# One operand's transpose moved from the matrix engine to the DMA crossbar, with three loads held behind it

## The chip, the cores and the metric

One core of a Trainium2 chip. The metric is the device time of one execution in microseconds (us). Several executions are compared; a run is slow when it is over 1.5% above the fastest of its kernel. A ratio is the mean time of one kernel's fast runs over that of the other's fast runs of the same rounds, so it is not quite the ratio of the medians quoted beside it. The span in a profile (248.2 us for the kernel before) is a little shorter than the device time of the same run (249.99 us). Places in time are us from the start of the span.

Engines: PE is the matrix engine, DVE the vector engine, ACT the scalar engine, POOL the general engine (here it issues the loads and does some copies), SP the engine that issues the transposing DMA transfers and the output stores. "SPq" in a profile line is an instruction of SP's DMA issue. SBUF is the on-chip memory that the engines work from, PSUM the one that PE writes its results to (psA and ot in the profile lines), and "the crossbar" is short for the way of a transposing transfer (DMA_TRANSPOSE in the profile lines). A transfer has landed when its completion is signalled.

## The reference

Two attentions, then a gated two-layer product. Shapes: 8 batches, 8 heads, 576 rows, head size 64, 32 packed queries; the second part is 4608 x 512 with a hidden size of 2048.

```python
def sm_attn(qq, kk, vv):                      # softmax(scale * qq kk^T) vv
    ...
p_packed = sm_attn(p, k, v)                   # first attention: 32 packed queries a head
out      = sm_attn(q, p_packed, p_packed)     # second attention: 32 keys a head
x = out.transpose(0, 2, 1, 3).reshape(4608, 512)
h = x @ w_in
result = (h * cos(h)) @ w_out
```

## The kernel before

The kernel works batch by batch. For batch b it needs k and q with the head dimension on the partitions ("kT", "qT"), so both are transposed after loading. This is done in one of two ways: on PE, in three groups of eight transposes, each group copied out of PSUM by DVE, or by a transposing DMA through the crossbar, issued from SP. The attention weights of the first attention ("a1") are transposed too, in the same two ways.

Loads are issued from POOL and convert fp32 to bf16 on the way. Each moves 576 KB into SBUF.

"Slot s" is the stretch in which the hidden products of batch s run on PE (16 steps, "fc"), filled up with the output products of batch s - 1. "Hooks" put other work at given steps. Between two slots stand the scores of the next batches.

```python
def load(n, b):                                   # POOL issues; bf16 in SBUF
    bf[n, b] = bf_pool.tile(..., bufs=2 if n == "k" else 1)
    G.dma_start(out=bf[n, b], in_=srcs[n][b]...)

def xbar(n, b):                                   # transposing DMA, SP issues
    t = xT[n, b] = att_pool.tile([128, H * 3, TP], ..., bufs=2 if n == "k" else 1)
    nc.sync.dma_start_transpose(out=t, in_=bf[n, b]...)

def pe_T(n, b, engs, groups, own=False):          # 8 PE transposes a group, 1 copy
    ...
# --- cut: set-up and batch 0 ---
    a1_one(1)
    load("k", 2)
    permute_v(1)
    load("v", 2)
    for fc in range(NFC):                         # slot 0
        ...
# --- cut ---
    def tk(n, b, i):
        return lambda: pe_T(n, b, (V, V, V), (i,))

    def next_loads():                             # the gate: POOL reads one element of kT3,
        G.tensor_copy(out=gate, in_=xT["k", 3][0:1, 0, 0:1])   # so it stops until kT3 landed
        for n, b in (("q", 3), ("k", 4), ("v", 3)):
            load(n, b)
    ...
    s2(1)
    ppw(1, 0, V)
    load("q", 2)
    load("k", 3)
    dup_p(4, 2 * B, G)
    ...
    slot(1, [(3, ...), (4, lambda: (xbar("q", 2), xbar("k", 3))),
             (5, tk("k", 2, 0)), (6, tk("k", 2, 1)), (7, tk("k", 2, 2)),
             (9, ...), (11, ...), (12, next_loads)], 4, {3: 3})
    ...
    # --- of this stretch only the lines that matter here; fillers and others are cut ---
    s1(2)              # first scores of batch 2: need kT2
    a1_pe(2, ...)      # its attention weights transposed on PE
    pp(2)              # its pooled product a1 x v: needs v2
    s2(2)              # second scores of batch 2: need qT2
    s1(3)              # first scores of batch 3: need kT3
    xbar("q", 3)       # three transfers, in this order on SP
    a1_xbar(3)
    xbar("k", 4)
    ...
    slot(2, [(4, lambda: permute_v(3, V)), (7, lambda: pp(3, ...)), (11, ...)], 5, {11: 3})
```

The pooled product of batch 3, pp(3), is in slot 2. It needs v3 (unpacked on DVE by permute_v(3)) and a1T3, the transposed attention weights of batch 3. From slot 3 on the kernel repeats one pattern.

The softmax here doesn't subtract the row's maximum and nothing guards it: scores larger than these inputs give would overflow.

Of the kernel before, what the change touches and what calls it, by code (L numbers as in the profile page):

```python
# [15 lines left out]
def kernel(  # L16
# [38 lines left out]
    V, ACT, G = nc.vector, nc.scalar, nc.gpsimd  # L55
# [5 lines left out]
    gate = const.tile([1, 1], BF16, name="gate")  # L61
# [8 lines left out]
    bf, vp, xT, a1T, sums1, r1, rs1 = {}, {}, {}, {}, {}, {}, {}  # L70
    a2u, lns, a2n, PPW = {}, {}, {}, {}

    def copy(eng, out, in_):
        if eng is ACT:
            ACT.copy(out=out, in_=in_)  # L75
        else:
            eng.tensor_copy(out=out, in_=in_)  # L77

    def psa(dt=FP32):
        return A.tile([128, 2, 512 if dt == FP32 else 1024], dt, name="psA", tag="A")  # L80

    def load(n, b):
        bf[n, b] = bf_pool.tile([TP, H, C * D], BF16, name=n + "bf", tag=n + "bf", bufs=2 if n == "k" else 1)
        G.dma_start(out=bf[n, b], in_=srcs[n][b].rearrange("h (p c) d -> p h (c d)", c=C))

    def permute_v(b, eng=G):
        vp[b] = vp_pool.tile([TP, C, H * D], BF16, name="vp", tag="vp")
        copy(eng, vp[b].rearrange("p c (h d) -> p c h d", h=H),
             bf["v", b].rearrange("p h (c d) -> p c h d", c=C))

    def xbar(n, b):
        t = xT[n, b] = att_pool.tile([128, H * 3, TP], BF16, name=n + "T", tag=n + "T", bufs=2 if n == "k" else 1)
        nc.sync.dma_start_transpose(out=t, in_=bf[n, b].rearrange("p h x -> p (h x)"))

    def pe_T(n, b, engs=(V, V, V), groups=(0, 1, 2), own=False):
        if 0 in groups:
            xT[n, b] = att_pool.tile([128, H * 3, TP], BF16, name=n + "T", tag=n + "T", bufs=2 if n == "k" else 1)
        t = xT[n, b]
        flat = bf[n, b].rearrange("p h x -> p (h x)")
        for i in groups:  # L100
            ps = bank(BF16) if own else psa(BF16)[:, 0, :]
            for j in range(8):
                o = 8 * i + j
                nc.tensor.transpose(ps[:, j * TP:(j + 1) * TP], flat[:, o * 128:(o + 1) * 128],  # L104
                                    ident[0:TP, 0:TP])
            copy(engs[i], t[:, 8 * i:8 * i + 8].rearrange("p a x -> p (a x)"),
                 ps[:, 0:8 * TP])

    def bank(dt=FP32):
        return O.tile([128, 512 if dt == FP32 else 1024], dt, name="ot", tag="ot")  # L110

    def pack_p(b0, b1, flat=None):
        ng = 2 * (b1 - b0)
        if flat is None:
            flat = psa(BF16).rearrange("p a x -> p (a x)")
        for g in range(ng):
            nc.tensor.transpose(flat[:, g * 128:(g + 1) * 128],
                                p_bf[:, 2 * b0 + g].rearrange("p t d -> p (t d)"), ident)
        V.tensor_copy(out=P2[:, b0:b1].rearrange("p b h n -> p (b h n)"), in_=flat[:, 0:ng * 128])
# [75 lines left out]
    def ppw(b, n, eng=None, own=False, later=False, cuts=((0, 512),)):  # L195
        if b not in PPW:
            PPW[b] = ppw_pool.tile([128, 2, DF], BF16, name="PPW", tag="PPW")
        two = isinstance(eng, tuple)
        if own:
            ps = [bank(), bank()]  # L200
        else:
            t = psa()
            ps = [t[:, 0, :], t[:, 1, :]]
        for x in range(4):
            for y in range(2):
                r = slice(64 * y, 64 * y + 64)
                nc.tensor.matmul(ps[y][32 * x:32 * x + 32, :], ppT[b % 2][r, 2 * x + y, :],  # L207
                                 w_in_bf[r, x, n * 512:(n + 1) * 512], start=True, stop=True)

        def evacuate(cuts=cuts):  # L210
            if own or two:
                for a, z in cuts:
                    for y in range(2):
                        copy(eng[y] if two else eng, PPW[b][:, y, n * 512 + a:n * 512 + z], ps[y][:, a:z])
            else:
                copy(eng or (V, ACT)[n % 2], PPW[b][:, :, n * 512:(n + 1) * 512], t)
        if later:
            return [lambda c=c: evacuate((c,)) for c in cuts]
        evacuate()
# [8 lines left out]
    def sums2(b, y):  # L228
        if b not in lns:
            lns[b] = att_pool.tile([128, 2, S], FP32, name="lns", tag="lns")  # L230
        ps = psa()
        for e in range(2):
            nc.tensor.matmul(ps[:, e, 0:HS], ones_blk, a2u[b][:, y, e * HS:(e + 1) * HS],  # L233
                             start=True, stop=True)
        ACT.activation(out=lns[b][:, y].rearrange("p (e x) -> p e x", e=2),  # L235
                       in_=ps[:, :, 0:HS], func=AF.Ln)
# [11 lines left out]
    def h_mm(b, fc):  # L248
        if fc == 0:
            gT[b] = g_pool.tile([128, NFC, S], BF16, name="gT", tag="gT")  # L250
            if b % 2 == 0:
                joint[b // 2] = j_pool.tile([128, NFC, 128], BF16, name="joint", tag="joint")
        ps = psa()
        for y in range(2):
            for e in range(2):
                nc.tensor.matmul(ps[:, e, 0:HS], PPW[b][:, y, fc * 128:(fc + 1) * 128],  # L256
                                 a2n[b][:, y, e * HS:(e + 1) * HS], start=(y == 0), stop=(y == 1))
        cs = cos_pool.tile([128, S], BF16, name="cosT")
        csv = cs.rearrange("p (e x) -> p e x", e=2)
        ACT.activation(out=csv, in_=ps[:, :, 0:HS], func=AF.Sin, bias=PI_HALF)  # L260

        def rest():
            V.tensor_tensor(out=gT[b][:, fc, :].rearrange("p (e x) -> p e x", e=2),  # L263
                            in0=ps[:, :, 0:HS], in1=csv, op=ALU.mult)
            if fc % 8 == 7:
                j0 = (b % 2) * 64
                G.tensor_copy(out=joint[b // 2][:, fc - 7:fc + 1, j0:j0 + 64],  # L267
                              in_=gT[b][:, fc - 7:fc + 1, 512:576])
        return rest
# [56 lines left out]
    def fill(n):  # L326
        while n > 0 and filler[1] > 0:
            next(filler[0])
            filler[1] -= 1
            n -= 1  # L330
# [9 lines left out]
    def dup_p(a, b, eng):  # L340
        for t in range(2):
            eng.tensor_copy(out=p_bf[:, a:b, t, :], in_=p_raw[:, a:b, :])
# [57 lines left out]
    a1_one(1)  # L400
    load("k", 2)
    permute_v(1)
    load("v", 2)
    for fc in range(NFC):
        rest = h_mm(0, fc)
        if fc in (11, 12, 13):
# [13 lines left out]
    def slot(s, hooks, keep=0, heavy={}):  # L420
        left = filler[1] - keep
        out_eng[:] = (ACT,) if s > 1 else (V, ACT)
        weight = [1 + heavy.get(fc, 0) for fc in range(NFC)]
        for fc in range(NFC):
            h_mm(s, fc)()
            quota = (left * sum(weight[:fc + 1])) // sum(weight) - (left + keep - filler[1])
            first = quota
            while hooks and hooks[0][0] == fc:
                if first == quota and fc in heavy:
                    first = quota // 2  # L430
                    fill(first)
                hooks.pop(0)[1]()
            fill(quota - first if first != quota else quota)

    def pw2(b, n=0, eng=None):
        ppw(b, n, eng)
        ppw(b, n + 1, eng)

    def tk(n, b, i):
        return lambda: pe_T(n, b, (V, V, V), (i,))  # L440

    def next_loads():
        G.tensor_copy(out=gate, in_=xT["k", 3][0:1, 0, 0:1])
        for n, b in (("q", 3), ("k", 4), ("v", 3)):
            load(n, b)
# [2 lines left out]
    fill(4)  # L448
    s2(1)
    ppw(1, 0, V)  # L450
    load("q", 2)
    load("k", 3)
    dup_p(4, 2 * B, G)
    fill(5)
    sums2(1, 0)
    sums2(1, 1)
# [2 lines left out]
    normalise(1)  # L459
    ACT.preload_act_table_set(SIN_SET)  # L460
    fill(14)
    slot(1, [(3, lambda: pw2(1, 2, (ACT, V))), (4, lambda: (xbar("q", 2), xbar("k", 3))), (5, tk("k", 2, 0)), (6, tk("k", 2, 1)),
             (7, tk("k", 2, 2)), (9, lambda: pack_p(2, 5)),
             (11, lambda: pack_p(5, B)), (12, next_loads)], 4, {3: 3})

    ACT.preload_act_table_set(EXP_SET)
# [104 lines left out]
```

## Time and profile before

| what | value | where read |
|---|---|---|
| time | 249.91 us (median of the first 3 runs; 6 runs later: 249.81 to 250.28) | times |
| PE busy | 94% of 248.2 us | busy shares |
| granted PE clock | 1.00 | mean of the core |
| DMA | a queue of loads until about 58 us, about 205 GB/s | 40 slices, landings |

The profile page of the kernel before: the busy row of PE, and of the 40 slices the granted clock (9 is 90% or more), the mean busy share of the DMA engines and the GB/s they moved. A slice is 6.2 us.

```profile
...
PE 234.5 (94%) x2003; PEld 131.6 (53%) x2037; DVE 168.0 (68%) x254; ACT 166.9 (67%) x278; POOL 54.8 (22%) x68
...
PEclk9999999999999999999999999999999999999999
DMA  6999999999899999999989995989491113201133
GB/s 91 203 203 206 205 206 229 200 241 153 162 206 219 167 158 220 206 193 173 190 162 192 174 194 68 177 164 209 103 156 33 45 42 82 47 26 58 46 83 85
...
```

PE is the limit. The DMA row reads 9 from the second slice to the tenth (about 62 us), and mostly 8 or 9 well beyond. k2, v2, q2 and k3 took 20.0, 19.4, 16.4 and 18.6 us from issue to landing and landed one after the other, the last at 58.6 us, while the trio after the next gate took 6.8 to 12.6 us. Up to about 58 us, then, loads stand in a queue. The transfers issued by SP (start, duration of the issue on SP, out<-in):

```profile
...
55.70 3.96 SPq L93 DMA_TRANSPOSE qT<-qbf  x1
59.72 2.94 SPq L93 DMA_TRANSPOSE kT<-kbf  x1
...
72.11 5.98 SPq L93 DMA_TRANSPOSE qT<-qbf  x1
78.19 2.46 SPq L156 DMA_TRANSPOSE a1T<-a  x1
...
```

An issue's duration is not its landing. The trace's issue-to-landing times say that qT2 landed 5.4 us after 55.70, kT3 4.9 us after 59.72, qT3 10.4 us after 72.11 (two loads were still under way beside it), and a1T3 5.6 us after 78.19, at 83.8. POOL's gate on kT3:

```profile
...
64.70 0.18 POOL L443 COPY gate<-kT 1x1 bf16<-1x1 bf16 x1 [8.52 <-DMA kT<-kbf]
...
```

It opened at 64.70. Then q3, k4 and v3 were issued, and landed at 72.0, 75.7 and 79.4.

PE's timeline. First steps with and without a group of transposes (L256 opens each step; L104 is a group):

```profile
...
46.02 0.65 PE L256 MATMUL psA<-a2n,PPW 128*128 128x288 bf16 x4
...
46.94 0.65 PE L256 MATMUL psA<-a2n,PPW 128*128 128x288 bf16 x4
...
51.90 0.65 PE L256 MATMUL psA<-a2n,PPW 128*128 128x288 bf16 x4
52.60 0.50 PE L104 MATMUL psA<-ident,kbf 96*128 96x96 bf16 x8
...
53.38 0.65 PE L256 MATMUL psA<-a2n,PPW 128*128 128x288 bf16 x4
...
```

From 46.02 to 46.94 a plain step takes 0.92 us; from 51.90 to 53.38 a step with a group takes 1.48 us. Then the points:

```profile
...
63.89 0.44 PE L129 MATMUL psA<-kT,P 64*32 64x288 bf16 x16
...
69.77 0.44 PE L129 MATMUL psA<-qT,ppT 64*32 64x288 bf16 x16
...
71.54 0.44 PE L129 MATMUL psA<-kT,P 64*32 64x288 bf16 x16
...
78.07 0.41 PE L256 MATMUL psA<-a2n,PPW 128*128 128x288 bf16 x2
...
85.58 0.86 PE L183 MATMUL psA<-a1T,vp 96*128 96x64 bf16 x24 [0.58 <-DVE gT L263]
...
```

These are the first scores of batch 2 (kT2), its second scores (qT2), the first scores of batch 3 (kT3), the first hidden product of slot 2, and pp(3). No DMA is waited for at any of them. a1T3 had landed at 83.8, so it had 1.8 us to spare at 85.58.

### The profile page before, as it was taken

The numbers are of one execution on the slowest core, as the hardware profiler recorded it, in microseconds if no ns is written. First come the engines' busy times: TensorE is split into PE (matmuls) and PEld (weight loads), VectorE is DVE, ScalarE is ACT, GpSimd is POOL, SyncE is SP. The second block draws the span as 40 slices with busy tenths as digits, with TensorE's granted clock in tenths as the row PEclk, the third lists the DMA queues.
The fourth block names the chain that finished last, engine by engine and source line by source line (L and its number), as shares of the span: only waits on it lengthen the run. The fifth ranks groups of instructions, "written<-read, shape, count | busy, mean of one in ns | idle before, by whom it ended". The sixth has DMA issues, their size and how long they took to land.

```text
span 248.2 us, 5035 instructions
## 1 busy us (share of the span) xinstructions
PE 234.5 (94%) x2003; PEld 131.6 (53%) x2037; DVE 168.0 (68%) x254; ACT 166.9 (67%) x278; POOL 54.8 (22%) x68
## 2 busy tenths in 40 slices
PE   8878799999999899999999999999999999999993
PEld 3454374566544654475546554565456554665452
DVE  2549987789568967678857766678766774876110
ACT  2368799746566787888877777888787684873000
POOL 8333533240400044022313105030500000000000
PEclk9999999999999999999999999999999999999999
DMA  6999999999899999999989995989491113201133
GB/s 91 203 203 206 205 206 229 200 241 153 162 206 219 167 158 220 206 193 173 190 162 192 174 194 68 177 164 209 103 156 33 45 42 82 47 26 58 46 83 85
DMA packets 63175, 37.09 MB, mean 149 GB/s; under 512 B 35792, under 2 KB 58576, under 8 KB 63152
## 3 DMA queue, kind: packets, MB, share of 16 engines
q0 software_dynamic: 23152, 18.75, 49.5%
q1 hardware_dynamic: 39568, 17.83, 34.3%
q8 instruction: 16, 0.26, 0.4%
q10 hardware_dynamic: 432, 0.20, 0.4%
q14 instruction: 7, 0.06, 0.1%
HBM read 37.22 MB, written 9.44 MB: 188 GB/s over the span
## 4 chain that ended last, share of the span: by engine, by line
PE 75%; DMA 9%; DVE 7%; ACT 5%; issue 2%; SPq 0%; DVEq 0%; ACTq 0%
PE ot L309 42%; PE psA L256 19%; DMA qbf<-in_q_dram 7%; DVE gT L263 4%; PE psA L207 3%; PE ot L347 3%; PE psA L183 2%; ACT cosT L260 2%; DMA out_dram<-osb 2%; PE psA L129 2%; PE ot L295 1%; PE psA L233 1%; DVE PPW L77 1%; ACT ppT L75 1%; PE psA L104 1%
## 5 line engine op out<-in xcount | busy, mean ns | idle before, releaser
L309 PE MATMUL ot<-w_out_bf,gT 128*128 128x512 bf16 x482 | 127.4, 379 | 2.1 <-issue 1.3
L263 DVE TENSOR_TENSOR gT<-psA,cosT 128x576 bf16<-128x576 f32 x128 | 93.6, 755 | 26.5 <-ACT cosT L260 25.9
L260 ACT ACTIVATE cosT<-psA 128x576 bf16<-128x576 f32 x128 | 82.5, 652 | 28.0 <-PE psA L256 23.2
L256 PE MATMUL psA<-a2n,PPW 128*128 128x288 bf16 x512 | 83.8, 286 | 1.9 <-DVE PPW L77 0.4
L309 PEld LDWEIGHTS <-gT 128*128 128x128 bf16 x512 | 47.7, 98 | 43.2 <-issue 6.7
L256 PEld LDWEIGHTS <-PPW 128*128 128x128 bf16 x512 | 49.3, 98 | 35.2 <-issue 4.4
L77 DVE CAST PPW<-psA 128x1024 bf16<-128x1024 f32 (+1 forms) x23 | 26.9, 1176 | 11.6 <-PE psA L207 11.5
L267 POOL COPY joint<-gT 128x512 bf16<-128x512 bf16 x16 | 9.8, 614 | 88.5 <-DVE gT L263 88.5
L77 DVE COPY osb<-ot 128x512 f32<-128x512 f32 (+1 forms) x24 | 16.3, 679 | 17.5 <-PE ot L309 7.6
L75 ACT COPY osb<-ot 128x512 f32<-128x512 f32 (+1 forms) x13 | 7.3, 565 | 15.3 <-PE ot L309 10.6
L77 POOL COPY vp<-vbf 96x3072 bf16<-96x3072 bf16 x6 | 16.5, 2751 | 3.8 <-DMA vbf<-in_v_dram 3.8
L243 DVE SCALAR_TENSOR_TENSOR a2n<-a2u,r,lns 128x576 bf16<-128x576 bf16 x16 | 12.3, 814 | 7.3 <-ACT lns L241 7.3
L140 ACT ACTIVATE a<-psA 128x576 bf16<-128x576 f32 x16 | 10.3, 647 | 7.1 <-PE psA L129 7.1
L235 ACT ACTIVATE lns<-psA 128x576 f32<-128x576 f32 x16 | 10.2, 650 | 7.1 <-PE psA L233 6.5
L309 PE MATMUL ot<-w_out_bf,joint 128*128 128x512 bf16 x46 | 12.4, 379 | 0.1
L225 ACT ACTIVATE a2u<-psA,rs 128x576 bf16<-128x576 f32 x16 | 11.0, 737 | 1.4 <-PE psA L129 1.3
L75 ACT CAST ppT<-psA 64x128 bf16<-64x128 f32 x24 | 6.2, 260 | 7.2 <-DVE ppT L77 5.9
L207 PE MATMUL psA<-w_in_bf,ppT 64*32 64x512 bf16 x224 | 10.2, 381 | 0.0
L347 PE MATMUL ot<-wz 128*128 128x512 bf16 x23 | 8.7, 524 | 1.4 <-DVE wz L358 1.2
L241 ACT ACTIVATE lns<-lns 128x576 f32<-128x576 f32 x16 | 10.0, 676 | 0.0
L183 PEld LDWEIGHTS <-vp 96*128 96x128 bf16 x192 | 6.6, 98 | 2.2 <-issue 1.1
L77 DVE COPY kT<-psA 128x768 bf16<-128x768 bf16 x8 | 4.2, 552 | 5.2 <-PE psA L104 5.1
(72 smaller groups left out, 150.8 us busy)
## 6 DMA issues: line engine op xcount, KB each, us to landing
kbf<-in_k_dram POOLq DMA_DIRECT2D x8, 576.0 KB, 12.0
vbf<-in_v_dram POOLq DMA_DIRECT2D x8, 576.0 KB, 7.3
qbf<-in_q_dram POOLq DMA_DIRECT2D x8, 576.0 KB, 9.6
out_dram<-osb SPq DMA_DIRECT2D x24, 192.0 KB, 2.6
out_dram<-osb SPq DMA_DIRECT2D x22, 128.0 KB, 2.4
w_in_bf<-in_moe_w_in_dram POOLq DMA_DIRECT2D x4, 512.0 KB, 17.5
w_out_bf<-in_moe_w_out_dram POOLq DMA_DIRECT2D x4, 512.0 KB, 20.4
out_dram<-osb SPq DMA_DIRECT2D x26, 64.0 KB, 2.1
```

The lines of the kernel that those rows point to most:

```text
L75: ACT.copy(out=out, in_=in_)
L77: eng.tensor_copy(out=out, in_=in_)
L140: ACT.activation(out=a1[b % 2][:, y, :, 0:TP].rearrange("p (e m) x -> p e m x", e=2), in_=ps[y][:, :, 0:HS].rearrange("p e (m x) -> p e m ...
L183: nc.tensor.matmul(ps[:, hp * 64:(hp + 1) * 64], vp[b][:, c, hp * 128:(hp + 1) * 128], a1T[b][0:TP, :, j, 32 * hp:32 * hp + 32], start=(j ...
L207: nc.tensor.matmul(ps[y][32 * x:32 * x + 32, :], ppT[b % 2][r, 2 * x + y, :], w_in_bf[r, x, n * 512:(n + 1) * 512], start=True, stop=True)
L225: ACT.activation(out=a2u[b][:, y].rearrange("p (e x) -> p e x", e=2), in_=ps[y][:, :, 0:HS], func=AF.Exp, scale=rs1[b][:, y:y + 1])
L243: V.scalar_tensor_tensor(out=a2n[b][:, y], in0=a2u[b][:, y], scalar=r1[b][:, y:y + 1], in1=lns[b][:, y], op0=ALU.mult, op1=ALU.mult)
L256: nc.tensor.matmul(ps[:, e, 0:HS], PPW[b][:, y, fc * 128:(fc + 1) * 128], a2n[b][:, y, e * HS:(e + 1) * HS], start=(y == 0), stop=(y == 1))
L260: ACT.activation(out=csv, in_=ps[:, :, 0:HS], func=AF.Sin, bias=PI_HALF)
L263: V.tensor_tensor(out=gT[b][:, fc, :].rearrange("p (e x) -> p e x", e=2), in0=ps[:, :, 0:HS], in1=csv, op=ALU.mult)
L309: nc.tensor.matmul(pss[c], w, w_out_bf[:, fc, :], start=(fc == 0), stop=(fc == NFC - 1))
L347: nc.tensor.matmul(wps, wz[:, 0:128], wz, start=True, stop=True)
```

## The change

The intent: take 24 transposes off PE, the busiest engine, and give k2 to the crossbar. The three following loads are held until that transfer has landed, in the way the kernel does it for later batches.

```diff
     load("k", 2)
     permute_v(1)
-    load("v", 2)
+    xbar("k", 2)
     for fc in range(NFC):
# --- cut ---
-    def tk(n, b, i):
-        return lambda: pe_T(n, b, (V, V, V), (i,))
# --- cut ---
     ppw(1, 0, V)
-    load("q", 2)
-    load("k", 3)
     dup_p(4, 2 * B, G)
+    G.tensor_copy(out=gate, in_=xT["k", 2][0:1, 0, 0:1])
+    for n, b in (("v", 2), ("q", 2), ("k", 3)):
+        load(n, b)
# --- cut ---
-    slot(1, [(3, ...), (4, lambda: (xbar("q", 2), xbar("k", 3))), (5, tk("k", 2, 0)), (6, tk("k", 2, 1)),
-             (7, tk("k", 2, 2)), (9, ...),
+    slot(1, [(3, ...), (4, lambda: (xbar("q", 2), xbar("k", 3))), 
+             (9, ...),
              (11, ...), (12, next_loads)], 4, {3: 3})
```

More of the change, by code (lines that the diff above doesn't have):

```diff
@@ L461 @@
     fill(14)
-    slot(1, [(3, lambda: pw2(1, 2, (ACT, V))), (4, lambda: (xbar("q", 2), xbar("k", 3))), (5, tk("k", 2, 0)), (6, tk("k", 2, 1)),
-             (7, tk("k", 2, 2)), (9, lambda: pack_p(2, 5)),
+    slot(1, [(3, lambda: pw2(1, 2, (ACT, V))), (4, lambda: (xbar("q", 2), xbar("k", 3))),
+             (9, lambda: pack_p(2, 5)),
              (11, lambda: pack_p(5, B)), (12, next_loads)], 4, {3: 3})
```

## The prediction

> **What bounds the kernel now.** The page's busy shares: PE 94% of 248.2 us, DVE 68%, ACT 67%; full clock. The chain of waits is 75% PE. But up to about 58 us the loads are a second limit: the DMA row of the 40 slices reads 9 without a break at about 205 GB/s, and the issue-to-landing times show a queue served in order: k2 (issued 28.4, +20.0) lands at 48.4, v2 at 51.6, q2 at 55.6, k3 at 58.6. The timeline of SP and POOL then shows qT2 transferred from 55.7 (+5.4), kT3 from 59.7 (+4.9), the gate opening at 64.7, and q3, k4, v3 landing at 72.0, 75.7, 79.4.
>
> **Removed.** 24 PE transposes in slot 1, in groups of 8 lasting 0.50 us (timeline of PE), and three DVE evictions of 0.55 us. A step of slot 1 with such a group takes 1.47 us, without 0.92: PE, the limit there, gains 3 x 0.55 = 1.65 us.
>
> **Added and moved.** One crossbar transfer of k2. v2, q2 and k3 no longer follow k2 in the queue: they start after kT2 has landed. [...] qT3, run beside two loads, landed after 10.4 us instead of 5.4. So the gate trades overlap for latency, where DMA has none to spare.
>
> Estimated from these durations:
> - kT2 lands at 48.4 + 4.9 = 53.3; gate opens 53.4.
> - v2, q2, k3 issued at 53.9, 54.7, 55.4. After later gates such a trio lands 6.5, about 9.3, about 12 us after issue: 60.4, 64.0, 67.4.
> - qT2 lands about 69.4. PE would ask for it (second scores of batch 2) at 69.8 - 1.65 = 68.1: waits 1.3.
> - kT3 starts when SP has issued qT2, at 68.0, and lands at 72.9 (before 64.6). First scores of batch 3, before at 71.5, are 1.4 late: the gain is gone.
> - The next gate opens 8.3 later. q3 lands at 80.3; SP's issue of qT3 beside two loads takes 6.0, then a1T3 is transferred and lands at about 91. The pooled product of batch 3 in slot 2 needs it; it ran at 85.6 with a slack under 2, and now PE is some 5.5 late there. v3 lands near 88, so the DVE copy that unpacks it (83.9 before) stalls too, inside the same wait.
> - In slot 3 q4 comes about 6.5 later, with a1T4 still in time; from slot 4 the DMA slack of about 5 absorbs the rest. PE's delay is never won back, since PE is the limit there.
>
> The delays are not a sum: the last and largest counts.
>
> **Predicted:** 249.9 + about 5 = 255 us, 8 in 10 within 251.5 to 258. Faster by over 2%: 0.04; within 2%: 0.45; slower by over 2%: 0.51.
>
> **What would show it.** Right: PE busy about 1.5 us less; slot 1 shorter by 1.65; DMA row dips near 50 us; gate near 53.4; kT3 landing near 73; new PE idle before the scores of batches 2 and 3, and several us at the pooled product of batch 3, released by a DMA (a1T or v). Wrong: no such idle, slot 2 starting on time.
>
> **What would make it wrong.** The k2 load landing earlier without v2 behind it, or faster loads and transfers once they no longer overlap: each us gained on that DMA chain is a us less stall, down to 248.3. The reverse if the transfers slow one another more.

## The result, and the profile after

257.34 us (median of 6 fast runs, 256.47 to 258.81) against 249.91 us (249.81 to 250.28). The ratio is 1.030, 95% interval 1.0268 to 1.0332: slower by 3.0%, inside the predicted range of 251.5 to 258. The profiled run took 256.47 us with a span of 254.7 us, 6.5 us more than before. The rest of this section explains those 6.5 us.

The same rows of the page, for the changed kernel (a slice is 6.4 us):

```profile
...
PE 238.0 (93%) x2013; PEld 130.9 (51%) x2013; DVE 166.8 (65%) x251; ACT 166.7 (65%) x278; POOL 54.9 (22%) x69
...
PEclk9999999999977999999999999999999999999999
DMA  6999999679979999999999992999291111302133
GB/s 88 203 204 205 206 206 226 88 146 208 200 187 168 219 177 146 229 206 172 209 210 187 169 220 72 156 199 185 84 196 44 41 44 41 82 6 60 59 82 82
...
```

The DMA row dips to 6 near 50 us (88 GB/s, slice 8, 44.6 to 50.9 us): there the end of k2's load, with nothing queued behind it, and then k2's transfer run alone. From 44.6 to 48.7, 53.7 and 57.3 us DMA moved 96, 154 and 89 GB/s, where the kernel before moved 210 GB/s from 48 to 58 us. New is the pair of 7 in the clock row, slices 12 and 13 (70 to 83 us). SP's transfers:

```profile
...
48.74 3.13 SPq L93 DMA_TRANSPOSE kT<-kbf  x1
...
63.84 3.80 SPq L93 DMA_TRANSPOSE qT<-qbf  x1
67.75 3.02 SPq L93 DMA_TRANSPOSE kT<-kbf  x1
...
81.31 6.03 SPq L93 DMA_TRANSPOSE qT<-qbf  x1
87.44 1.46 SPq L156 DMA_TRANSPOSE a1T<-a  x1
...
```

The gates of POOL:

```profile
...
53.77 0.18 POOL L449 COPY gate<-kT 1x1 bf16<-1x1 bf16 x1 [5.77 <-DMA kT<-kbf]
54.29 0.77 POOL L84 DMA_DIRECT2D vbf<-in_v_dram  x1 [0.34 <-POOL gate L449]
...
74.44 0.18 POOL L440 COPY gate<-kT 1x1 bf16<-1x1 bf16 x1 [10.13 <-DMA kT<-kbf]
...
```

The gate on kT3 opens at 74.44 instead of 64.70. Everything behind it on the DMA side moves: qT3's issue from 72.11 to 81.31, a1T3's from 78.19 to 87.44. a1T3 landed 4.6 us after its issue, at 92.0; that is 8.2 us later than before, and less the 1.8 us that it had to spare it makes 6.4 us. PE's timeline at the same points as before:

```profile
...
62.20 0.44 PE L129 MATMUL psA<-kT,P 64*32 64x288 bf16 x16
...
69.23 0.44 PE L129 MATMUL psA<-qT,ppT 64*32 64x288 bf16 x16 [1.08 <-DMA qT<-qbf]
...
74.36 0.68 PE L129 MATMUL psA<-kT,P 64*32 64x288 bf16 x16 [3.30 <-DMA kT<-kbf]
...
83.62 0.41 PE L256 MATMUL psA<-a2n,PPW 128*128 128x288 bf16 x2
...
92.16 0.86 PE L183 MATMUL psA<-a1T,vp 96*128 96x64 bf16 x24 [1.60 <-DMA a1T<-a]
...
```

| point on PE | before | after | after - before | waited for |
|---|---|---|---|---|
| first scores of batch 2 | 63.89 | 62.20 | -1.69 | |
| second scores of batch 2 | 69.77 | 69.23 | -0.54 | qT2, 1.08 |
| first scores of batch 3 | 71.54 | 74.36 | +2.82 | kT3, 3.30 |
| slot 2 begins | 78.07 | 83.62 | +5.55 | |
| pp(3) | 85.58 | 92.16 | +6.58 | a1T3, 1.60 |
| end of span | 248.2 | 254.7 | +6.5 | |

The removed transposes did give PE 1.69 us. Then PE falls behind at every further point up to pp(3), and after that nothing is added or won back: from there to the end it is 162.6 us before and 162.5 us after.

Between 74.36 and 83.62 PE waits for nothing, yet it needs 9.26 us for what took 6.53 us before (71.54 to 78.07). The view of windows shows why. Its columns: window, its length, busy time of PE, weight load, DVE, ACT and POOL with instruction counts, granted clock, DMA share (a sum of packet times, so it can exceed 1), GB/s. Two windows of the changed kernel:

```profile
...
74.36:83.62 9.26, 9.17 (x66) 3.41 (x66) 4.86 (x7) 4.99 (x9) 3.09 (x5) 0.69 1.03 164
83.60:92.20 8.60, 6.65 (x45) 4.16 (x45) 7.54 (x11) 5.53 (x9) 0.00 (x0) 1.00 1.24 202
...
```

And the same work in the kernel before:

```profile
...
71.50:78.07 6.57, 6.33 (x66) 2.86 (x67) 4.83 (x8) 5.02 (x10) 0.00 (x0) 1.00 1.27 217
...
```

In short windows the granted clock is 0.50 from 73.33 to 80.16 us. PE's wait for kT3 had begun at about 71.1. The clock thus fell 2.3 us into the wait (it was 1.00 until then: window 71.10:73.33, with no matmul in it) and stayed at half for 6.83 us, some 1.0 us of it still in the wait. Why it fell then and not at once, or came back at 80.16, this trace does not show.

So two accounts of the 6.5 us are possible, and they overlap in time:

- Theory A, the DMA chain. k2's transfer and the gate delay v2, q2, k3; these delay qT2 and kT3; that delays the gate on kT3, q3, qT3's issue, and a1T3 behind it on SP. pp(3) starts when a1T3 lands, whatever PE did before.
- Theory C, the clock. PE idled for 3.30 us, the clock was 0.50 for 6.83 us, and PE lost 2.7 us (9.26 us instead of 6.53).
- Theory B concerns the part inside A: is it the gate that costs (DMA at 89 to 154 GB/s instead of 210), or the transfer itself?

### The profile page after: what moved, and what is told of

Its sections match the earlier page's. It is cut to its first block, busy times and chain, and to the rows that moved or that the text cites. A ratio compares the mean times of both kernels' runs of the same rounds, so it can differ in the third digit from the quotient of the medians.

```text
span 254.7 us, 5024 instructions
## 1 busy us (share of the span) xinstructions
PE 238.0 (93%) x2013; PEld 130.9 (51%) x2013; DVE 166.8 (65%) x251; ACT 166.7 (65%) x278; POOL 54.9 (22%) x69
## 4 chain that ended last, share of the span: by engine, by line
PE 70%; DMA 19%; DVE 4%; ACT 2%; issue 2%; POOL 2%; SPq 0%; DVEq 0%; POOLq 0%
PE ot L309 42%; PE psA L256 19%; DMA w_out_bf<-in_moe_w_out_dram 8%; DMA w_in_bf<-in_moe_w_in_dram 6%; PE psA L207 3%; DMA kT<-kbf 3%; DVE gT L263 2%; DMA a1T<-a 2%; PE psA L183 2%; PE psA L129 2%; PE ot L295 1%; PE psA L233 1%; ACT cosT L260 1%; DVE PPW L77 1%; ACT ppT L75 1%
## 5 line engine op out<-in xcount | busy, mean ns | idle before, releaser
L309 PE MATMUL ot<-w_out_bf,gT 128*128 128x512 bf16 x512 | 135.0, 384 | 0.1
L309 PEld LDWEIGHTS <-gT 128*128 128x128 bf16 x512 | 48.2, 98 | 44.7 <-issue 8.4
L309 PE MATMUL ot<-w_out_bf,joint 128*128 128x512 bf16 x48 | 12.8, 379 | 0.0
L207 PE MATMUL psA<-w_in_bf,ppT 64*32 64x512 bf16 x224 | 10.6, 394 | 0.0
L129 PE MATMUL psA<-kT,P 64*32 64x288 bf16 x128 | 4.4, 306 | 3.6 <-DMA kT<-kbf 3.3
```

The source lines that it names most:

```text
L207: nc.tensor.matmul(ps[y][32 * x:32 * x + 32, :], ppT[b % 2][r, 2 * x + y, :], w_in_bf[r, x, n * 512:(n + 1) * 512], start=True, stop=True)
L309: nc.tensor.matmul(pss[c], w, w_out_bf[:, fc, :], start=(fc == 0), stop=(fc == NFC - 1))
```

## The experiments

There were twelve runs, of eleven kernels. All gave correct results, beside runs of the kernel before on the same chip. A summary first. "pp(3)" is where pp(3) starts in the profiled run, "rest" is the span minus that.

| run | time, median (range) | ratio to before | gate on kT3 | pp(3) | rest |
|---|---|---|---|---|---|
| before | 249.91 (249.81 to 250.28) | | 64.70 | 85.58 | 162.6 |
| changed kernel | 257.34 (256.47 to 258.81) | 1.0300 | 74.44 | 92.16 | 162.5 |
| e1 no gate | 257.39 (257.01 to 257.82) | 1.0296 | 71.38 | 90.70 | 165.2 |
| e2 hold only | 252.84 (251.05 to 253.64) | 1.0104 | 67.82 | 88.17 | 162.6 |
| e3 crossbar only | 252.98 (251.82 to 255.03) | 1.0104 | 68.23 | 88.73 | 164.6 |
| e4 changed + dummy matmuls | 259.25 (257.94 to 260.04) | 1.0365 | 73.22 | 92.98 | 164.2 |
| e5 e3 + a1T first | 254.41 (249.68 to 257.05) | 1.0073 fast runs | 67.75 | 84.93 | 162.6 |
| e6 before + a1T first | 249.93 (249.86 to 250.28) | 0.9993 | 64.63 | 85.55 | 162.7 |
| e7 changed + a1T first | 258.11 (256.61 to 259.58) | 1.0316 | 73.64 | 90.61 | 164.2 |
| e8 e3 + dummy matmuls | 253.01 (252.22 to 253.47) | 1.0109 | 68.28 | 87.91 | 162.5 |
| e9 e5 + v3 first | 253.03 (248.56 to 254.65) | 0.9935 fast runs | 67.83 | 85.78 | 162.5 |
| e10 e7 + v3 first | 256.93 (254.38 to 260.39) | 1.0187 fast runs | 74.43 | 91.27 | 165.1 |
| e11 e9, a1 of batch 3 on PE | 249.40 (249.15 to 249.89) | 0.9976 | 67.52 | 84.94 | 162.7 |

Before's median was 249.91 to 250.22 us in these rounds. Differences under 2% count as no change: the changed kernel, e1, e4 and e7 are slower, e10 is unclear, all others are the same. Times are medians of all runs. Where the ratio says "fast runs", the slow runs left out may be slow by the kernel's own doing, so the ratio flatters these kernels; read the range beside it.

Two things stand out. First, every profiled run is pp(3) plus a constant. Second, the constant has two values: 162.5 to 162.7, and 164.2 to 165.2. The second group (e1, e3, e4, e7, e10) is just those profiles in which a stretch at half clock lies after pp(3) or reaches past it.

### e1: the changed kernel without the gate

```diff
-    G.tensor_copy(out=gate, in_=xT["k", 2][0:1, 0, 0:1])
     for n, b in (("v", 2), ("q", 2), ("k", 3)):
         load(n, b)
```

> The changed kernel without the gate's copy: k2 still goes by the crossbar, v2, q2 and k3 are issued by POOL right after the duplication of p, estimated near 48.0 us (there POOL ended it in the changed kernel) instead of 54.3. Theory A (the DMA chain k2 -> v2,q2,k3 -> qT2,kT3 -> gate -> q3 -> qT3 -> a1T3 sets the time, and a crossbar transfer costs its 5 us of that chain whether gated or not): the gate before q3 opens about 3 us earlier than in the changed kernel, near 71.5, and the time is about 254. Theory B (what costs is the gate's idle queue alone; transfers overlap with loads nearly for free): gate near 68.5, time 250 to 251. Theory C (the loss is the lowered TensorE clock after PE's wait): no matter for the gate, time falls only if PE's wait before the first scores of batch 3 (3.3 us) goes away.

Measured: 257.39 us, ratio 1.0296; no faster than the changed kernel. The loads were issued from 47.64, and the gate on kT3 opened at 71.38, as theory A had it (71.5). k2's transfer landed 15.1 us after its start, beside the three loads, instead of 5.0 us alone. Then PE stood for a1T3:

```profile
...
90.70 1.44 PE L183 MATMUL psA<-a1T,vp 96*128 96x64 bf16 x24 [5.87 <-DMA a1T<-a]
...
```

pp(3) started 1.5 us earlier than in the changed kernel, but half clock (89.4 to 96.2) now reached past it and the rest grew by 2.7 us (165.2 against 162.5). The expected 254 us missed that. The gate is thus a part of the cost and not all of it. With it the gate on kT3 opened 9.74 us late, without it 6.68 us; of the 3.06 us between, 1.46 us reached pp(3), and half clock after pp(3) took them back. The larger part stays without the gate, since the transfer and the loads beside it took longer together (k2's transfer 15.1 us instead of 5.0 us, k3's load 13.6 us to land instead of 10.8 us). Theory B as stated (gate near 68.5, 250 to 251 us) is refuted.

### e2: the hold without the crossbar

```diff
     permute_v(1)
-    load("v", 2)
 ...
-    load("q", 2)
-    load("k", 3)
     dup_p(4, 2 * B, G)
+    G.tensor_copy(out=gate, in_=bf["k", 2][0:1, 0, 0:1])
+    for n, b in (("v", 2), ("q", 2), ("k", 3)):
+        load(n, b)
```

(on the kernel before, PE transposes kept)

> The kernel before, with its PE transposes of k2, but v2, q2 and k3 are held by a gate on the landing of k2 itself, no crossbar transfer of k2. Issued near 49, they should land near 55.7, 58.5, 61.5, so 3 us later than before (k3 58.6) and 5 us earlier than in the changed kernel. Theory A: gate before q3 near 67.7 (64.7 before, 74.4 changed), no PE wait at the scores of batch 3, a wait of about 1 us at the pooled product of batch 3 because its slack was under 2 us: time about 251 (250.3 to 252). If the PE transposes were what mattered, or the crossbar alone, this equals before: 249.9.

Measured: 252.84 us, ratio 1.0104 (1.0061 to 1.0146), 0.8 us above the expected range. The gate on kT3 opened at 67.82 (expected 67.7).

```profile
...
88.17 0.86 PE L183 MATMUL psA<-a1T,vp 96*128 96x64 bf16 x24 [3.22 <-DMA a1T<-a]
...
```

A shift of the gate by 3.1 us moved pp(3) by 2.6 us, more than the 1.3 us that are left of it after the slack of 1.8 us: q3 took 9.5 us to land instead of 6.8 us. Holding three loads by some 3 us costs 1% (the interval excludes no change, though it is under the 2% rule) with PE's work unchanged. Nothing here needs the crossbar or the removed transposes.

### e3: the crossbar without the hold

```diff
     permute_v(1)
     load("v", 2)
+    xbar("k", 2)
 ...
-             (5, tk("k", 2, 0)), (6, tk("k", 2, 1)), (7, tk("k", 2, 2)),
```

(on the kernel before)

> k2 by a crossbar transfer and no PE transposes in slot 1, but v2, q2, k3 issued where the kernel before issues them (32, 39, 40 us), no gate. Theory A [...]: k3 lands 3 to 5 us later than before, gate near 68.5, the saved 1.65 us of PE is lost again at the pooled product of batch 3: time 249.9 to 252. Theory B (the gate is all of the loss): gate near 65, time 248.3.

Measured: 252.98 us, ratio 1.0104 (1.0059 to 1.0149), the upper end of theory A's range exceeded by 1 us. The profiled run is the slowest of the four (255.03 us). The gate opened at 68.23 (A: 68.5; B: 65), but not in the way that theory A had it. kT2 landed 12.0 us after its start, beside the loads; the loads, however, were hardly delayed: q2 landed at 55.1 and k3 at 59.4, against 55.6 and 58.6 before, where 3 to 5 us later was expected of k3. What came late is SP, whose issues follow one another in the program's order. The stores of the kernel before:

```profile
...
47.14 2.05 SPq L316 DMA_DIRECT2D out_dram<-osb  x4
...
```

and SP in e3:

```profile
...
48.58 7.00 SPq L93 DMA_TRANSPOSE kT<-kbf  x1
55.62 3.83 SPq L316 DMA_DIRECT2D out_dram<-osb  x4
59.56 3.27 SPq L93 DMA_TRANSPOSE qT<-qbf  x1
...
```

The issue of k2's transfer held SP for 7.0 us beside the loads (3.13 us in the changed kernel, with no load beside it). The four stores stood behind it, and qT2 was issued 4.4 us after q2 had landed. So theory A's number was met by luck. Whether qT2 issued ahead of the stores would win this back was not tested. In the changed kernel the chain does run as theory A has it: q2 landed at 63.7 and qT2 was issued at 63.84.

PE reached slot 2 early, and lost all of it at pp(3):

```profile
...
88.73 1.44 PE L183 MATMUL psA<-a1T,vp 96*128 96x64 bf16 x24 [5.25 <-DMA a1T<-a]
...
```

This is the smallest form of the change, and it still loses: the transfer, 12.0 us beside the loads instead of 5.0 us, holds up the transfers behind it on SP. The delays of the gate on kT3 fit together: 3.12 us by the hold alone (e2), 3.53 us by the crossbar alone (e3), 6.68 us by both (e1), and 9.74 us with POOL's gate on top.

### e4: PE kept busy in the changed kernel's waits

```diff
     fill(7)
+    warm(5)              # matmuls on zeros
     s2(2)
     ppw(2, 0, V)
     fill(5)
+    warm(15)
     s1(3)
```

(on the changed kernel)

> The changed kernel with 5 and 15 matmuls on zeros put where PE waits for qT2 (1.1 us) and kT3 (3.3 us), so that PE is not idle there. Theory A: the granted clock stays at 1.00 between 74 and 81 us, PE reaches slot 2 some 2.5 us earlier, but then waits that much longer for a1T3, which lands near 92 all the same: time unchanged within 0.5 us, about 257. Theory C (the lowered clock after PE's wait is what costs): time falls by about 2.5 us to 254.7.

Measured: 259.25 us, no faster. Between 74 and 81 us the clock stayed at 1.00. The dummies were somewhat too many: the first scores of batch 3 started at 76.36, although kT3 had landed by 73.2. Even so PE stood before pp(3) at about 89.8 us, 0.7 us earlier than in the changed kernel, and waited longer:

```profile
...
92.98 0.86 PE L183 MATMUL psA<-a1T,vp 96*128 96x64 bf16 x24 [3.16 <-DMA a1T<-a]
...
```

pp(3) did not start earlier (92.98 against 92.16), as theory A says. Half clock then came after pp(3), 94.5 to 97.9, and the rest grew to 164.2. Theory C fails for the changed kernel: its 2.7 us at half clock lay in the shadow of a1T3. In these runs half clock cost time only where no DMA wait followed to hide it: the rest was 162.5 us in the changed kernel and 164.2 us here.

### e5 and e6: the order on SP

```diff
-    xbar("q", 3)
     a1_xbar(3)
+    xbar("q", 3)
 ...
-            xbar("q", s + 1)          # and so in every later slot
         fill(10)
 ...
             a1_xbar(s + 1)
+            xbar("q", s + 1)
```

e5 is e3 with this edit, e6 the kernel before with it.

> As e3 (k2 by the crossbar, loads as before, no gate), and on SP the transfer of the first-attention weights a1T is issued ahead of the transfer of q in every slot, so that it no longer waits for q3's load and for SP's 6 us issue of qT3. Theory A: in slot 2 the pooled product of batch 3 finds a1T3 there (landing near 78 instead of 88), the 5.3 us wait goes, the granted clock stays at 1.00, the saved PE transposes are kept: about 248 us (247.5 to 248.8), below both kernels. If something else than a1T3 holds that product (v3, or the q3 chain itself), it waits still and the time stays at 250 or more.

> The kernel before with only the order of a1T and qT on SP changed, as in e5. The pooled product of batch 3 waits there 0.6 us for DVE, for no DMA, so by theory A little is to be had: 249.3 to 250.0, the same within 0.3 percent.

e6 measured 249.93 us, ratio 0.9993 (0.9981 to 1.0005): as expected, there was nothing to win there.

e5 had a profiled run of 249.68 us with pp(3) at 84.93, but its other runs took 250.9, 253.1, 255.7, 256.6 and 257.1 us, so the expected 248 us was missed. The last three are listed as slow (over 1.5% above the fastest). Mean clocks went down to 0.986; no run of the kernel before was under 0.993. What pp(3) waited for in the profiled run was DVE, and DVE was waiting for v3:

```profile
...
83.25 0.96 DVE L77 COPY vp<-vbf 96x3072 bf16<-96x3072 bf16 x1 [0.62 <-DMA vbf<-in_v_dram]
...
```

The same kernel later:

> The kernel of e5 once more, for another look: five of its six runs were slower than the profiled one, by up to 7 us. Theory: if this look is a slow one, PE waits over 3 us before the pooled product of batch 3, released by DVE behind the load of v3, and the clock falls to 0.5 after it. If it waits elsewhere, the spread has another cause.

Of the waits seen until then, those of 3.30 us (changed kernel), 5.87 us (e1) and 5.25 us (e3) came with half clock, and one of 3.22 us (e2) did not.

It took 249.02 us, with pp(3) at 84.55 and a 1.0 us wait behind DVE there. It was again a good run, and could not show where the slow ones wait.

### e7: the same order in the changed kernel

The edit of e5 on the changed kernel, gate and all.

> The changed kernel, gate and all, with the same reordering on SP. Theory A: the waits for qT2 (1.1 us) and kT3 (3.3 us) and the lowered clock after them stay, since they come earlier; the 1.6 us wait for a1T3 goes: about 255.5. If the whole loss were the a1T3 wait, it would fall to 249.

Measured: 258.11 us, against an expected 255.5. pp(3) came 1.5 us earlier (90.61), held now by DVE behind v3, which landed at 88.9. But the 2.0 us of idle PE before it were followed by half clock after it (92.1 to 95.5), and the rest grew by 1.7 us. a1T3, issued at 75.35 just as the loads of q3, k4 and v3 began, landed 13.7 us later.

### e8: dummy matmuls where the wait is the last link

```diff
-             (7, lambda: pp(3, engs=(ACT, ACT)))
+             (7, lambda: (warm(22), pp(3, engs=(ACT, ACT))))
```

(on e3)

> As e3, with 22 matmuls on zeros just before the pooled product of batch 3 in slot 2, in the place of its 5.3 us wait for a1T3. Theory: the clock is lowered because PE is idle, and where the wait is the last link nothing hides that. The product starts when it did in e3 (near 88.7), but the granted clock stays at 1.00 and the about 2 us after it are saved: median near 251.3, every run with a mean clock of 0.997 or more. If the lowered clock has another cause [...], the time and the clock stay as in e3.

Windows around pp(3), first e3:

```profile
...
84.00:86.00 2.00, 0.00 (x0) 0.00 (x0) 1.95 (x3) 0.17 (x1) 0.00 (x0) 1.00 1.91 197
86.00:88.00 2.00, 0.00 (x0) 0.00 (x0) 1.00 (x2) 0.00 (x0) 0.00 (x0) 0.50 0.79 161
88.00:90.00 2.00, 1.27 (x25) 1.30 (x26) 0.00 (x0) 0.00 (x0) 0.00 (x0) 0.50 1.20 250
90.00:92.00 2.00, 2.00 (x11) 1.00 (x9) 0.00 (x0) 1.04 (x4) 0.18 (x1) 0.50 0.75 160
...
```

and e8:

```profile
...
84.00:86.00 2.00, 2.00 (x11) 0.91 (x10) 2.00 (x4) 0.01 (x1) 0.00 (x0) 1.00 0.48 102
86.00:88.00 2.00, 2.00 (x13) 0.94 (x12) 0.03 (x1) 0.00 (x0) 0.00 (x0) 1.00 1.19 247
88.00:90.00 2.00, 1.94 (x34) 1.49 (x34) 0.00 (x0) 1.13 (x5) 0.00 (x0) 1.00 1.10 192
90.00:92.00 2.00, 2.00 (x16) 1.36 (x14) 1.40 (x2) 1.74 (x3) 0.33 (x2) 1.00 0.83 197
...
```

The granted clock is the third number from the right: 0.50 in e3, 1.00 in e8, and the rest is 162.5 instead of 164.6. All four runs of e8 had a mean clock of 0.996 to 1.0, all four of e3 0.986 to 0.993. So the clock fell where PE stood idle before pp(3), and stayed at 1.00 with the same burst of matmuls when dummies filled the wait. The time, however, did not fall: 253.01 against 252.98 us. Two runs of e3 (251.82 and 251.97) were faster than any of e8. A likely reason is that the 22 dummies occupy PE for 4.9 us (PE's timeline of e8, from 83.16) even in runs where a1T3 comes early; no profile shows such a run. In the profiled run they were already a little too many: a1T3 had landed at 87.6, and pp(3) started at 87.91.

### e9 and e10: v3 first

```diff
-        for n, b in (("q", 3), ("k", 4), ("v", 3)):
+        for n, b in (("v", 3), ("q", 3), ("k", 4)):
```

e9 is e5 with this edit, e10 is e7 with it.

> As e5, with v3 loaded first of the three loads of slot 1 (v3, q3, k4 instead of q3, k4, v3). In e5's profiled run the unpacking of v3 waited 0.6 us for its load; the other runs of e5 were slower with a lower mean clock. Theory: in those v3 came later still, PE stood over 3 us and the clock fell; with v3 first (landing near 75, needed at 82.6) nothing on the DMA chain holds slot 2, PE keeps the 1.65 us of removed transposes, and the runs agree with one another: 247.9 to 248.6, mean clock 0.997 or more. If the slower runs of e5 have another cause, the spread of 250 to 257 stays.

> The changed kernel, gate and all, with a1T ahead of qT on SP and v3 first of the loads of slot 1, so that neither holds the pooled product of batch 3. Theory: the 2.0 us that e7's profile shows there go, the waits for kT3 and the lowered clock before it stay: about 2 us under e7, so 255 to 256. The rest over the kernel before (about 5 us) is then the kT3 wait (3.6) and the lowered clock (2 to 3), less the 1.65 of removed transposes. If more than that goes, or nothing, the two waits in slot 2 were not what they seem.

e9's fast runs took 248.56, 248.60 and 250.37 us (ratio 0.9935, 0.9918 to 0.9952), the four others 253.0 to 254.7 us. The spread stayed, so v3 was not its cause alone. In the profiled run v3 landed early, at 75.4, and now a1T3 held pp(3) by 2.3 us, though issued 14 us before. The view of the tile a1T in that stretch, with its last line for the landing:

```profile
...
L156 SPq DMA_TRANSPOSE a1T<-a x1: 4269/4269/4269, 71.8 to 71.8; - x1
...
DMA to landing us min/median/max: 13.8/13.8/13.8
```

e10's fast runs took 254.38 and 255.36 us (ratio 1.0187; the verdict is unclear, with only two of four runs fast). One is a little under the expected 255 to 256, one within. Its profile fell on a slow run: there a1T3 landed 15.0 us after its issue, pp(3) waited 3.45 us for it, and half clock set in during that wait (89.9 to 96.8). That is the one look at a slow run of this family.

So the same transfer of a1T takes 4.6 us when it runs alone at the end of the chain (changed kernel), 7.2 us when two loads are still under way (e6), and 11.4 to 15.0 us when it is issued beside three (e5, e5b, e7, e9, e10). The order on SP had been hiding this. Beside three it took 2.5 to 3.3 times the 4.6 us. No run here shows how the engines are shared between the transfers, so the size stays unexplained.

### e11: no DMA between the scores and pp(3)

```diff
-    a1_xbar(3)
     xbar("q", 3)
     recips(3)
     xbar("k", 4)
     fill(5)
     sums2(2, 0)
+    a1_pe(3, (0,))       # 6 PE transposes and a DVE copy
     sums2(2, 1)
+    a1_pe(3, (1,))
     fill(3)
```

(on e9)

> As e9 (k2 by the crossbar, no gate, a1T ahead of qT on SP from slot 3 on, v3 first), but the attention weights of batch 3 are transposed on PE (12 transposes, two evictions on DVE, as the kernel does for batch 2) instead of by the crossbar. In e9's profiled run that crossbar transfer, issued at 71.8 beside three loads, landed 13.8 us later and held the pooled product of batch 3 by 2.3 us. Theory: with no DMA between the scores and the pooled product of batch 3 this wait is gone in every run, and with it the spread and the lowered clock. PE gets 1.65 us and gives back about 0.7: 248.8 to 249.4, all runs within 0.6 us, mean clock 0.997 or more. If the spread of e5 and e9 (248.6 to 257) stays, it does not come from that wait.

Measured: 249.40 us, six runs from 249.15 to 249.89 us, mean clocks 0.997 to 1.0; before in the same rounds 249.95 us. The ratio is 0.9976, interval 0.9958 to 0.9994: faster by a quarter of a percent, which is far within the 2% that would count as a change. The spread is gone.

```profile
...
84.94 0.86 PE L183 MATMUL psA<-a1T,vp 96*128 96x64 bf16 x24 [0.58 <-DVE gT L263]
...
```

pp(3) waits as long as before, for the same DVE product. The saving of PE is what is left: 1.65 us from k2, less about 1.0 us for a1 (from the first scores of batch 3 to the double group of products with w_in, L207 x16, that follows: 3.90 us here and 2.91 us before). That leaves some 0.65 us; the medians differ by 0.55 us.

## Why the prediction was right or wrong, point by point

- Direction and size: right. Slower, 257.34 us against 255 us, in the range; it leaned to slower by over 2% with 0.51, hardly more than even.
- Transposes removed give PE 1.65 us in slot 1: right, 1.69 us.
- "PE busy about 1.5 us less": wrong as a sign. The page shows 238.0 us against 234.5 us. It counts half-clock matmuls as longer (L129 of the first scores of batch 3: 430 ns, before 288 ns), and the trace before lacks 30 of the 512 L309 records with gT (x482, against x512 after). Busy time of PE was a bad witness.
- kT2 at 53.3, gate at 53.4, DMA dip near 50 us: right (gate 53.77).
- qT2 about 69.4, wait 1.3 us: right (69.0 and 1.08 us).
- kT3 at 72.9, scores of batch 3 late by 1.4 us: right in kind, too small. kT3 took 6.6 us to land instead of the 4.9 us used, and the scores were 2.8 us late. Output stores were issued right behind it (from 70.87 us), as they were before (from 62.76 us); what made it longer was not found.
- The gate 8.3 us later: 9.74 us.
- The last link counts, not the sum; it is pp(3), behind a1T3: right. Its delay was 6.58 us, predicted 5.5 us. Shown by the same rest of 162.5 us in both kernels and by e1 to e4. In e11 taking a1T3 off the DMA removed the loss, but e11 is built on e9, without the gate; the same edit on the changed kernel, where kT3's wait would remain, was not run. e10, with both holds on pp(3) moved, had fast runs of 254.4 and 255.4 us, so most of the loss stays there.
- "PE's delay is never won back", "a1T4 still in time": right.
- v3 late, stalling DVE inside the same wait: wrong here. v3 landed at 87.4 but its copy ran at 89.47 without a wait, since slot 2 itself was late. It showed in e5 and e7.
- "Several us at the pooled product": only 1.6 us of idle there. The rest of the delay had been taken up earlier, by 3.3 us for kT3 and by half clock.
- Missing altogether: the lowered clock. In the changed kernel it is hidden by a1T3 (e4), so the sum came out nearly right without it, which is luck in part: in e4, where the waits of the scores were filled, another stretch fell after pp(3) and did count. In e1, e3 and e7 it is in the open and cost 1.7 to 2.7 us, and my expectations of those runs failed by it.
- "Faster loads and transfers once they no longer overlap" as the way to be wrong: this is the trade that e1 measured. Gated, k2's transfer took 5.0 us instead of 15.1 us, but the gate on kT3 opened later. Neither form wins. k2's load did not land earlier without v2 behind it (48.7 us, before 48.4).

Left open: why unprofiled runs of the changed kernel are up to 2.3 us slower than the profiled one, and where the slow runs of e5 and e9 wait. e10's slow profile and e11's steadiness point to a1T3 beside the loads, together with half clock after it; no profile of a slow run of e5 or e9 shows it. The mean clocks bound the clock's share, by an estimate from the stretches seen: 3.41 us at half clock lower the mean of a run by 0.007 and cost at most 1.7 us. The three slow runs of e5 had 0.987, so at most about 3.4 us of their 6.0 to 7.4 us over the profiled run; the rest must be waiting.

## What to carry to other kernels

Moving work from the busiest engine to DMA was not free here. Three things to check elsewhere: whether DMA has room at that moment (here loads stood in a queue until 58.6 us, at about 205 GB/s); whether the engine that issues the transfer is held up with other issues behind it (in e3 the issue took 7.0 us instead of 3.13 us); and whether something later hangs on the transfers behind it (a1T3 came 8.2 us later and had 1.8 us to spare). Follow the chain of transfers to the compute that uses the last one, and compare the shift with the slack there. Ask what a wait of a few us on PE does to its clock (here 0.50 for 3.41 or 6.83 us in or after waits of 2.0 to 5.87 us, not each time), and whether a later wait hides that. A short transfer that the next product needs should not be issued beside large loads (a1T: 4.6 us without, 11.4 to 15.0 us beside three); if PE can do it for about 1 us, as here, that is steadier.

## What the runs show of transfers and of the clock

- A transposing DMA beside loads gave correct results in all runs, but took longer. Measured, issue to landing: the k transfer 5.0 us alone, 12.0 us (e3) and 15.1 us (e1) beside loads; the a1 transfer 4.6 us with no load beside it, 7.2 us beside two, 11.4 to 15.0 us beside three. The issue itself got longer too: the k transfer's held SP for 3.1 us alone, 7.0 us (e3) and 9.2 us (e1) beside loads.
- The granted clock had two levels in these runs, 1.00 and 0.50. The low stretches lasted 3.41 us (e4, and two in e7) or 6.83 us (changed kernel, e1, e3, e10). They were of the longer kind when they began during the wait, and of the shorter when they began after PE had resumed, some 1.5 us later. The length of a wait did not decide it alone: half clock followed one of 2.0 us in e7 and did not come with one of 2.3 us in e9; one of 3.3 us lowered the clock in the changed kernel and one did not in e10 (for kT3); of two waits of 3.2 us one did (e4) and one did not (e2). So in these runs a wait of 2 to 3.3 us sometimes cost and sometimes did not, which may be part of the spread from run to run.
- Half clock cost nothing where a later DMA wait ended at the same time anyway: 2.7 us of it were hidden in the changed kernel, while in e1, where it lay after the last wait, the rest of the run grew by 2.7 us.
